# Hash-masked attention and two feed-forward blocks: the first head's operands loaded twice and written by the engines

## The chip, the cores and the metric

The kernel runs on one core of a Trainium2 chip. The core has TensorE (PE in the profile), VectorE (DVE), ScalarE (ACT), GpSimd (POOL) and SyncE (SP), each with its own instruction stream, and 16 DMA engines. Here SP and ACT issue the DMAs; the profile calls their queues q1 and q10. The metric is the device time of one execution in microseconds. The kernel before took 683.12 us (median of 3 runs, 682.26 to 685.02).

## The reference

All is computed in float32; some weights come as float64 and are converted in the kernel. Shapes: batch 2, 8 heads, 768 positions, 64 per head; model width 512.

```
q_bits = (q @ proj > 0);  k_bits = (k @ proj > 0)          # proj: 64 x 6, six sign bits
mask   = q_bucket[:, None] == k_bucket[None, :]            # the six bits as one number
scores = where(mask, q @ k.T / 8, -1e9)
attn   = exp(scores - max);  attn /= sum(attn) + 1e-9
x      = attn @ v                                          # 2 x 768 x 512, heads side by side
h = relu(x @ w_in);  u, v = halves of h;  v = layernorm(v)
y = (u * (w_spatial @ v + b_spatial)) @ w_out
out = y + relu(layernorm(y) * g_ln @ w_ch1) @ w_ch2
```

## The kernel before

TensorE multiplies float32 values in the format fp32r, and most operands are held as a pair, a high part (the value rounded to fp32r) and a low part (the rest), so that a product takes two or three passes.

Attention goes head by head. Two heads make a pair (`pair_load`, line 651): their keys and queries are loaded as 128 rows (two heads of 64) by 768 columns. `mismatch` (line 681) multiplies the raw pair by `sides`, a small matrix of `proj` with both signs (line 588), on PE into `pm`, and VectorE turns the signs into the mask rows `m`. `pair_split` (line 663) makes high and low parts. `passes_of` (line 703) assembles the operands of a single head: `ks`, 128 rows by two passes by 768 columns, and `qs`, the same by 384 columns (a group of three query tiles). Rows 0 to 63 and 64 to 127 hold different parts of the same head, and the second pass ends in 12 rows of mask. `passes_of` fills them by DMA from SBUF to SBUF; for the first head only, the mask rows are cast by VectorE (`first=True`). Then, for each tile of 128 queries: `scores` (four matmuls over 768 keys), `masked_max` on VectorE, `exps` on ScalarE, `transposes` on PE with copies `e` back to SBUF, and, per group, `weighted` (the product with the values `vv`).

Beside the attention, `conversions` loads float64 weights in pieces of 512 KB on ScalarE's queue (`stage_f64`: `f_out`, `f_v`, `f_u`) and converts them on ScalarE, VectorE and GpSimd. The first feed-forward block of batch 0 (`moe1`) lies in the attention's last part, and the rest of both blocks follows it.

The order is not written by hand. `Plan` records every operation as a job; `run` (line 281) simulates the engines with the costs in `cost` (line 220) and two DMA queues, twelve rounds, and `issue` emits the best order in time. A change of one job's cost or one job's place can thus reorder instructions far away. All recorded operations show line 478 of the profile's kernel (480 after the change).

Ahead of the first scores the kernel issues warming transposes of the identity matrix (`WARM` and `WARM2`, 24 and 12; their results are not used).

Of the kernel before, what the change touches and what calls it, by code (L numbers as in the profile page):

```python
# [9 lines left out]
F32 = mybir.dt.float32  # L10
F32R = mybir.dt.float32r
# [154 lines left out]
class Plan:  # L166
# [7 lines left out]
    LOOK = 60  # L174
    EARLY = 20.0
    ROUNDS = 12
    HOP = {"PE": 0.15, "ACT": 0.06, "DVE": 0.06, "POOL": 0.06, "SP": 0.05}
# [42 lines left out]
    def cost(self, engine, op, writes, reads, kw, job):  # L220
# [10 lines left out]
        if engine == "PE":  # L231
            if op == "transpose":
                return 0.109, 0.165
            if reads[0].dtype == F32:
                return n * (0.00083 if out.rows == 64 else 0.00042) + 0.006 + (0 if job.calls else 0.2), 0.2
            return n * 0.4375e-3 + 0.0065, 0.17
# [44 lines left out]
    def run(self, late=None):  # L281
# [20 lines left out]
        def opened(j):  # L302
            i = bisect_left(reached, j.at - self.LOOK)
            if i == len(reached):
                return None
            return max(when[i], late[j] - self.EARLY) if late else when[i]

# [176 lines left out]
def attn_moe_kernel(ctx: ExitStack, tc: tile.TileContext, qT, kT, v, proj, w_in, w_spT, b_sp, w_out, g_ln, w1, w2, out):  # L484
# [28 lines left out]
    WSE = (5, 3)  # L513
    WARM = 24
    WARM2 = 12
    XB = 3
# [65 lines left out]
    pj = const.tile([P, NB], F32, name="pj")  # L582
    nc.sync.dma_start(out=pj, in_=proj.rearrange("(o d) n -> o d n", o=1).to_broadcast([2, D, NB]))

# [5 lines left out]
    for a, own in enumerate((slice(0, D), slice(D, P))):  # L590
        for i, sign in enumerate((1.0, -1.0, 1.0)):
            at = a * HROW + i * NB
            nc.gpsimd.tensor_scalar(sides[own, at : at + NB], pj[own], sign, 0.0, op0=ALU.mult, op1=ALU.add)
    side = {"k": sides[:, NB : NB + QUAD], "q": sides[:, 0:QUAD]}
# [107 lines left out]

    def passes_of(nm, b, h, sl, first):

# [14 lines left out]
        for lo, hi in ((0, GW), (GW, S)):  # L719
            lo, hi = max(sl.start, lo), min(sl.stop, hi)  # L720
            if lo < hi:
                at = (2 * "kq".index(nm) + lo // GW) * QUAD + h % 2 * HROW
                rows = pr["m"][at : at + NM, lo % GW : lo % GW + hi - lo].bitcast(F32)
                to = t[D:MR, 1, lo - sl.start : hi - sl.start]
                if first:
                    nc.vector.tensor_copy(to, rows)
                else:
                    nc.sync.dma_start(out=to.bitcast(F32), in_=rows)
        return t

    def head_prep(b, h, first=False):
        heads[b, h] = {"ks": passes_of("k", b, h, slice(0, S), first)}

# [4 lines left out]

    def group_prep(b, h, g, first=False):
        groups[b, h, g] = {"qs": passes_of("q", b, h, slice(g * GW, (g + 1) * GW), first)}  # L740

# [335 lines left out]
    if WARM:  # L1077
        warm = ps_b.tile([P, P], F32, tag="b", name="warm")
        for _ in range(WARM):
            nc.tensor.transpose(warm, ident, ident)  # L1080
    pair_load(0, 0, first=True)
    mismatch(0, 0)
    pair_split(0, 0, first=True)
    head_prep(0, 0, first=True)
    group_prep(0, 0, 0, first=True)
    for _ in range(WARM2):
# [218 lines left out]
```

## Time and profile before

| | |
|---|---|
| time of the profiled execution | 684.13 us |
| its span, first to last instruction | 682.3 us |
| median of 3 runs (lowest, highest) | 683.12 us (682.26, 685.02) |
| busy: PE, DVE, ACT, POOL | 660.7, 433.0, 301.8, 197.2 us |
| mean granted clock of TensorE | 0.992 of 2.4 GHz |
| DMA | 84.36 MB, mean 124 GB/s |

A row of a timeline gives the start in us from the span's start, the length, the engine (a `q` behind the name: its DMA issues), and in brackets how long the engine had been idle and what ended that. Matmul lengths are latencies; several overlap. A row of stretches gives busy time per engine (PE, weight loads, DVE, ACT, POOL, each with a count), the granted clock, the busy share of the 16 DMA engines, and GB/s.

### The profile page before, as it was taken

The page shows a single profiled execution, that of the slowest core. Times are in us where ns is not written, and L with a number is a line of the kernel's source. Part 1 is how long each engine was busy: PE and PEld are TensorE (multiplying, and loading weights), DVE is VectorE, ACT ScalarE, POOL GpSimd, SP SyncE. Part 2 cuts the span into 40 slices and gives each one's busy share as a digit, 9 for nine tenths or more (in the row PEclk, how much of TensorE's full clock was granted, in tenths as well). Part 3 has the DMA queues.
Part 4 walks back from the last instruction along what each step waited for, and adds up shares of the span by engine and source line. Part 5 has one row for each costly group of instructions (what it writes and reads, how often), then busy time and mean ns, then how long its engine had stood idle before and what let it go on. Part 6 is the DMA issues. An engine that isn't in the chain of part 4 may idle for free. (4 is left out here: it accounts for less than half of the span.)

```text
span 682.3 us, 10207 instructions
## 1 busy us (share of the span) xinstructions
PE 660.7 (97%) x3772; PEld 537.6 (79%) x3772; DVE 433.0 (63%) x802; ACT 301.8 (44%) x591; POOL 197.2 (29%) x189
## 2 busy tenths in 40 slices
PE   6999999999999999999999999899999999999997
PEld 5887777878888788887688788688888878888886
DVE  2879787988657554534799686799888861112112
ACT  1887787767555545533464333433333221111110
POOL 2333433344432521100244241154554430000000
PEclk9899999999999999999999999899999999999999
DMA  7585765757546742624525440732332310002001
GB/s 195 133 212 139 186 176 147 191 122 193 175 92 218 217 117 73 226 121 162 186 80 216 137 133 33 263 113 89 106 92 93 93 61 1 0 1 92 1 1 61
DMA packets 47546, 84.36 MB, mean 124 GB/s; under 512 B 5678, under 2 KB 32010, under 8 KB 46474
## 3 DMA queue, kind: packets, MB, share of 16 engines
q1 hardware_dynamic: 34458, 54.36, 28.2%
q10 hardware_dynamic: 13040, 29.36, 13.2%
q8 instruction: 30, 0.49, 0.3%
q14 instruction: 18, 0.15, 0.1%
HBM read 51.12 MB, written 12.58 MB: 93 GB/s over the span
## 5 line engine op out<-in xcount | busy, mean ns | idle before, releaser
L478 PE MATMUL pc<-xh,w1t 128*128 128x512 f32 x576 | 143.9, 396 | 0.2 <-DVE xh L478 0.2
L478 PE MATMUL acc<-w2t,ch 128*128 128x512 f32 x576 | 141.9, 393 | 0.4 <-POOL w2t L478 0.4
L478 PEld LDWEIGHTS pc<-xh,w1t 128*128 128x128 f32 x576 | 108.4, 189 | 25.9 <-DVE xh L478 0.9
L478 PEld LDWEIGHTS acc<-w2t,ch 128*128 128x128 f32 x576 | 107.8, 188 | 25.0 <-POOL w2t L478 0.7
L478 ACT ACTIVATE x<-x,nb 128x768 f32<-128x768 f32 x96 | 89.6, 934 | 42.1 <-DVE x L478 38.2
L478 PE MATMUL sc<-ks,qs 128*128 128x512 f32 (+3 forms) x384 | 97.4, 372 | 7.7 <-DMA qs<-q 6.3
L478 DVE TENSOR_SCALAR_CACHE_REDUCE x<-sc 128x768 f32<-128x768 f32 x96 | 91.2, 953 | 19.5 <-PE sc L478 12.3
L478 DVE SCALAR_TENSOR_TENSOR ch<-pc,ch 128x512 fp32r<-128x512 f32 x48 | 33.0, 688 | 104.9 <-ACT ch L478 104.7
L478 PE MATMUL pt<-ident,x 128*128 128x128 f32 x576 | 82.7, 275 | 0.8 <-ACT e L478 0.5
L478 ACT ACTIVATE ch<-pc 128x512 fp32r<-128x512 f32 x48 | 28.7, 597 | 123.8 <-PE pc L478 123.4
L478 PEld LDWEIGHTS sc<-ks,qs 128*128 128x128 f32 (+1 forms) x384 | 65.2, 196 | 21.9 <-DMA qs<-q 7.2
L478 PEld LDWEIGHTS pt<-ident,x 128*128 128x128 f32 x576 | 66.9, 141 | 13.2 <-issue 3.1
L478 PE MATMUL po<-e,vv 128*64 128x192 f32 x768 | 69.5, 330 | 1.1 <-ACT e L478 1.1
L478 ACT ACTIVATE e<-pt 128x384 f32<-128x384 f32 x120 | 56.0, 484 | 31.4 <-PE pt L478 30.5
L478 POOL TENSOR_TENSOR f64c_w<-f_w,f64c_w 128x512 f32<-128x512 f32 x32 | 44.5, 1392 | 74.3 <-DVE f64c_w L478 70.9
L478 PEld LDWEIGHTS po<-e,vv 128*64 128x64 f32 x768 | 52.3, 137 | 12.4 <-issue 2.2
L478 DVE COPY e<-pt 128x384 f32<-128x384 f32 x72 | 39.7, 553 | 28.0 <-PE pt L478 27.7
L478 DVE TENSOR_SCALAR f64c_w<-f64c_w 128x512 f32<-128x512 f32 x64 | 40.7, 636 | 12.4 <-ACT f64c_w L478 11.4
L478 ACT ACTIVATE f64c_w<-f_w 128x512 f32<-128x512 f32 x32 | 21.5, 672 | 57.0 <-DMA f_w<-in_w 53.5
L478 PE MATMUL pg<-vn,w_sp 128*128 128x512 f32 x180 | 44.5, 399 | 0.0
L478 PEld LDWEIGHTS pg<-vn,w_sp 128*128 128x128 f32 x180 | 33.1, 188 | 8.0 <-issue 0.6
L478 DVE SCALAR_TENSOR_TENSOR f_w<-f_w,f64c_w 128x512 uint32<-128x512 uint32 x32 | 37.2, 1161 | 0.7
(125 smaller groups left out, 788.3 us busy)
## 6 DMA issues: line engine op xcount, KB each, us to landing
f_w<-in_w ACTq DMA_DIRECT2D x32, 512.0 KB
ks<-k SPq DMA_DIRECT2D x48, 192.0 KB
qs<-q SPq DMA_DIRECT2D x32, 192.0 KB
wst_sp<-in_w_spT SPq DMA_DIRECT2D x12, 384.0 KB
w_out<-ws_out SPq DMA_DIRECT2D x2, 2048.0 KB
qs<-q SPq DMA_DIRECT2D x32, 96.0 KB
vv<-in_v SPq DMA_DIRECT2D x16, 192.0 KB
ot<-y_dram SPq DMA_DIRECT2D x12, 256.0 KB
```

Source lines behind the costliest of these rows:

```text
L478: getattr(getattr(nc, engine[j.engine]), op)(*map(live, args), **{k: live(x) for k, x in kw.items()})
```

## The change

For the first head the parts are no longer copied from SBUF to SBUF. A new tile `dup` is loaded from DRAM: in its upper 64 partitions the first head's keys, and in both halves the first group's queries. ScalarE, VectorE and GpSimd write `ks` and `qs` in place from `k_raw` and `dup` (`first_parts`). The projection `pj` is issued by ScalarE instead of SyncE, and `sides` is written by VectorE instead of GpSimd. There are 24 warming transposes instead of 36, and the planner's cost of one is 0.213 instead of 0.109. A large DMA on ScalarE's queue may not be planned before 14.0 us (`BULK`).

```
@@ -173,6 +173,7 @@
     EARLY = 20.0
+    BULK = 14.0
     ROUNDS = 12
     HOP = {"PE": 0.15, "ACT": 0.06, "DVE": 0.06, "POOL": 0.06, "SP": 0.05}
     NEXT = 0.03
@@ -230,7 +231,7 @@
         psum = any(isinstance(x, View) and x.base.ring.pool.psum for x in (out, *reads))
         if engine == "PE":
             if op == "transpose":
-                return 0.109, 0.165
+                return (0.109 if isinstance(reads[0], View) else 0.213), 0.165
             if reads[0].dtype == F32:
                 return n * (0.00083 if out.rows == 64 else 0.00042) + 0.006 + (0 if job.calls else 0.2), 0.2
             return n * 0.4375e-3 + 0.0065, 0.17
@@ -303,7 +304,8 @@
             i = bisect_left(reached, j.at - self.LOOK)
             if i == len(reached):
                 return None
-            return max(when[i], late[j] - self.EARLY) if late else when[i]
+            bulk = self.BULK if j.engine == "ACT" and j.bytes > 200000 else 0.0
+            return max(when[i], bulk, late[j] - self.EARLY) if late else max(when[i], bulk)
 
         def done(j):
             stack = [j]
@@ -511,8 +513,8 @@
     VNP = [(0, t) for t in range(6)]
     UAT = {1: (0,), 2: (1,), 3: (2,), 5: (3, 4, 5)}
     WSE = (5, 3)
-    WARM = 24
-    WARM2 = 12
+    WARM = 16
+    WARM2 = 8
     XB = 3
     AT = (-10, -7, -6, -4, 0)
     PO = 2
@@ -580,7 +582,7 @@
     NM = 2 * NB
     MR = D + NM
     pj = const.tile([P, NB], F32, name="pj")
-    nc.sync.dma_start(out=pj, in_=proj.rearrange("(o d) n -> o d n", o=1).to_broadcast([2, D, NB]))
+    nc.scalar.dma_start(out=pj, in_=proj.rearrange("(o d) n -> o d n", o=1).to_broadcast([2, D, NB]))
 
 
     HROW = 3 * NB
@@ -590,7 +592,7 @@
     for a, own in enumerate((slice(0, D), slice(D, P))):
         for i, sign in enumerate((1.0, -1.0, 1.0)):
             at = a * HROW + i * NB
-            nc.gpsimd.tensor_scalar(sides[own, at : at + NB], pj[own], sign, 0.0, op0=ALU.mult, op1=ALU.add)
+            nc.vector.tensor_scalar(sides[own, at : at + NB], pj[own], sign, None, op0=ALU.mult)
     side = {"k": sides[:, NB : NB + QUAD], "q": sides[:, 0:QUAD]}
 
     above = const.tile([P, 1], F32, name="above")
@@ -700,7 +702,7 @@
     groups = {}
     tiles = {}
 
-    def passes_of(nm, b, h, sl, first):
+    def passes_of(nm, b, h, sl):
 
 
 
@@ -722,22 +724,48 @@
                 at = (2 * "kq".index(nm) + lo // GW) * QUAD + h % 2 * HROW
                 rows = pr["m"][at : at + NM, lo % GW : lo % GW + hi - lo].bitcast(F32)
                 to = t[D:MR, 1, lo - sl.start : hi - sl.start]
-                if first:
-                    nc.vector.tensor_copy(to, rows)
-                else:
-                    nc.sync.dma_start(out=to.bitcast(F32), in_=rows)
+                nc.sync.dma_start(out=to.bitcast(F32), in_=rows)
         return t
 
-    def head_prep(b, h, first=False):
-        heads[b, h] = {"ks": passes_of("k", b, h, slice(0, S), first)}
+    def first_load():
+        dup = ap.tile([P, NKT, GW], F32, tag="e", name="dup", bufs=EB)
+        nc.sync.dma_start(out=dup[D:P, 0:2], in_=kT[0, 0].rearrange("d (a s) -> d a s", a=2))
+        nc.sync.dma_start(
+            out=dup[:, 2], in_=qT[0, 0, :, 0:GW].rearrange("(o d) s -> o d s", o=1).to_broadcast([2, D, GW])
+        )
+        return dup
+
+    def first_parts(dup):
+        pr = pairs[0, 0]
+        k_raw = pr["k", "raw"]
+        ks = ap.tile([P, 2, S], F32R, tag="ks", name="ks_0_0_0", bufs=2)
+        qs = ap.tile([P, 2, GW], F32R, tag="qs", name="qs_0_0_0", bufs=QB)
+        nc.scalar.activation(ks[0:D, 1], k_raw[0:D], AF.Copy)
+        nc.vector.tensor_tensor(ks[0:D, 0], k_raw[0:D], ks[0:D, 1].bitcast(F32), op=ALU.subtract)
+        split_hi(ks[D:P, 0].rearrange("d (a s) -> d a s", a=2), dup[D:P, 0:2])
+        nc.scalar.activation(qs[:, 0], dup[:, 2], AF.Copy, scale=-SCALE)
+        nc.vector.scalar_tensor_tensor(
+            qs[D:P, 0], dup[D:P, 2], -SCALE, qs[D:P, 0].bitcast(F32), op0=ALU.mult, op1=ALU.subtract
+        )
+        nc.vector.tensor_copy(qs[0:D, 1], qs[0:D, 0])
+        heads[0, 0], groups[0, 0, 0] = {"ks": ks}, {"qs": qs}
+        for n, to in enumerate((ks[D:MR, 1, 0:GW], ks[D:MR, 1, GW:S], qs[D:MR, 1])):
+            rows = pr["m"][n * QUAD : n * QUAD + NM].bitcast(F32)
+            if n == 1:
+                nc.scalar.activation(to, rows, AF.Copy)
+            else:
+                nc.vector.tensor_copy(to, rows)
+
+    def head_prep(b, h):
+        heads[b, h] = {"ks": passes_of("k", b, h, slice(0, S))}
 
     def head_prep3(b, h):
         vv = ap.tile([P, NKT, D], F32, tag="vv", name=f"vv_{b}_{h}", bufs=2)
         nc.sync.dma_start(out=vv, in_=v[b, :, h])
         heads[b, h]["vv"] = vv
 
-    def group_prep(b, h, g, first=False):
-        groups[b, h, g] = {"qs": passes_of("q", b, h, slice(g * GW, (g + 1) * GW), first)}
+    def group_prep(b, h, g):
+        groups[b, h, g] = {"qs": passes_of("q", b, h, slice(g * GW, (g + 1) * GW))}
 
     def scores(b, h, g, j):
         jm = f"{b}_{h}_{g}_{j}"
@@ -1079,10 +1107,10 @@
         for _ in range(WARM):
             nc.tensor.transpose(warm, ident, ident)
     pair_load(0, 0, first=True)
+    dup = first_load()
     mismatch(0, 0)
+    first_parts(dup)
     pair_split(0, 0, first=True)
-    head_prep(0, 0, first=True)
-    group_prep(0, 0, 0, first=True)
     for _ in range(WARM2):
         nc.tensor.transpose(warm, ident, ident)
     head_prep3(0, 0)
```

The planner then orders VectorE's first instructions differently. Before, in the stretch up to the first masked maximum (`x`); `k_0_0` and `q_0_0` are the pair's split parts, `ks`, `qs` the first head's operands:

```order
L478 SCALAR_TENSOR_TENSOR k_0_0_144<-k_raw,k_0_0_144 128x768
L478 SCALAR_TENSOR_TENSOR q_0_0_158<-q_raw,q_0_0_158 128x768
L478 TENSOR_SCALAR m_0_179<-pm_0_172,above,worth 128x384
L478 CAST ks_0_0_154<-m_0_179 12x384 x2
L478 CAST qs_0_0_166<-m_0_179 12x384
L478 TENSOR_SCALAR x_0_0_0_199,nb_0_0_0_198<-sc_0_0_0_189 128x768
```

After:

```order
L480 TENSOR_SCALAR sides<-pj 64x6 x6
L480 SCALAR_TENSOR_TENSOR q_0_0_141<-q_raw,q_0_0_141 128x768
L480 TENSOR_TENSOR ks_0_0_157<-k_raw,ks_0_0_157 64x768
L480 TENSOR_SCALAR m_0_172<-pm_0_159,above,worth 128x384
L480 SCALAR_TENSOR_TENSOR qs_0_0_151<-dup,qs_0_0_151 64x384
L480 COPY qs_0_0_151<-qs_0_0_151 64x384
L480 CAST ks_0_0_157<-m_0_172 12x384
L480 CAST qs_0_0_151<-m_0_172 12x384
L480 SCALAR_TENSOR_TENSOR k_0_0_165<-k_raw,k_0_0_165 128x768
L480 TENSOR_SCALAR x_0_0_0_193,nb_0_0_0_192<-sc_0_0_0_183 128x768
```

`sides` and three instructions that write the first head's parts have come in; the split of the queries now stands ahead of that of the keys, which has gone behind the casts.

SyncE's queue from its first issue. Before (`qs_0_384` is the second query group of the first head, `ks_1_0` the second head's keys):

```order
L478 DMA k_raw<-in_kT 128x768
L478 DMA q_raw<-in_qT 128x768
L478 DMA pj<-in_proj 128x1x6
L478 DMA ks_0_0_154<-k_0_0_144 64x768 x3
L478 DMA qs_0_0_166<-q_0_0_158 64x2x384
L478 DMA qs_0_384_169<-q_0_0_158 64x2x384
L478 DMA qs_0_0_166<-q_0_0_158 64x384
L478 DMA qs_0_384_169<-q_0_0_158 64x384
L478 DMA ks_1_0_181<-k_0_0_144 64x768
L478 DMA qs_0_384_169<-m_0_179 12x384
L478 DMA ks_1_0_181<-k_0_0_144 64x768 x2
L478 DMA ks_1_0_181<-m_0_179 12x384 x2
```

After:

```order
L480 DMA q_raw<-in_qT 128x768
L480 DMA k_raw<-in_kT 128x768
L480 DMA dup<-in_qT 128x1x384
L480 DMA dup<-in_kT 64x768
L480 DMA vv_0_127<-in_v 128x384
L480 DMA qs_0_384_152<-q_0_0_141 64x2x384
L480 DMA qs_0_384_152<-q_0_0_141 64x384
L480 DMA ks_1_0_170<-k_0_0_165 64x768 x2
L480 DMA qs_0_384_152<-m_0_172 12x384
L480 DMA ks_1_0_170<-m_0_172 12x384 x2
L480 DMA ks_1_0_170<-k_0_0_165 64x768
L480 DMA q_0_1_198<-in_qT 128x768
```

The copies into `ks_0_0` and `qs_0_0` are gone, the two loads into `dup` and the value load stand ahead of all copies, and `pj` has left the queue.

ScalarE's queue up to the second `e` copy. Before:

```order
L478 ACT_TABLE_LOAD
L478 ACTIVATE k_0_0_144<-k_raw 128x768
L478 ACTIVATE q_0_0_158<-q_raw 128x768
L478 DMA f_out_210<-in_w_out 128x1024
L478 ACTIVATE x_0_0_0_199,z_sum_214<-x_0_0_0_199,nb_0_0_0_198 128x768
L478 ACTIVATE x_0_0_1_205,z_sum_214<-x_0_0_1_205,nb_0_0_1_204 128x768
L478 ACTIVATE x_0_0_2_222,z_sum_214<-x_0_0_2_222,nb_0_0_2_221 128x768
L478 ACTIVATE e_0_0_254<-pt_0_0_0_0_230 128x3x128
```

After:

```order
L480 DMA pj<-in_proj 128x1x6
L480 ACT_TABLE_LOAD
L480 ACTIVATE q_0_0_141<-q_raw 128x768
L480 ACTIVATE ks_0_0_157<-k_raw 64x768
L480 ACTIVATE k_0_0_165<-k_raw 128x768
L480 ACTIVATE qs_0_0_151<-dup 128x384
L480 ACTIVATE ks_0_0_157<-m_0_172 12x384
L480 ACTIVATE x_0_0_0_193,z_sum_206<-x_0_0_0_193,nb_0_0_0_192 128x768
L480 ACTIVATE x_0_0_1_201,z_sum_206<-x_0_0_1_201,nb_0_0_1_200 128x768
L480 ACTIVATE e_0_0_228<-pt_0_0_0_0_219 128x3x128
L480 DMA f_out_238<-in_w_out 128x1024
L480 ACTIVATE x_0_0_2_216,z_sum_206<-x_0_0_2_216,nb_0_0_2_215 128x768
```

The `pj` load comes first, three copies for the first head have come in, and the first weight load (`f_out`) has moved behind two exponentials and an `e` copy.

## Rows read from the trace of the kernel before

**Rows 1.** The page: TensorE's busy time; its granted clock in 40 slices:

```profile
PE 660.7 (97%) x3772; PEld 537.6 (79%) x3772; DVE 433.0 (63%) x802; ACT 301.8 (44%) x591; POOL 197.2 (29%) x189
...
PEclk9899999999999999999999999899999999999999
```

**Rows 2.** TensorE's waits, whole run: total, times, longest (us):

```profile
PE sc L478 <- DMA qs<-q: 6.3, 2, 5.3
PE px_c L478 <- ACT xc L478: 2.8, 1, 2.8
```

**Rows 3.** TensorE's timeline: start, length, instruction, count, idle before:

```profile
1.45 6.78 PE L478 MATMUL warm<-ident 128*128 128x128 f32 x36 [1.45 <-POOL above L478]
8.16 0.52 PE L478 MATMUL pm<-k_raw,sides 128*32 128x384 f32 x2
...
14.31 5.64 PE L478 MATMUL sc<-ks,qs 128*128 128x512 f32 x16 [5.30 <-DMA qs<-q]
19.75 1.21 PE L478 MATMUL pt<-ident,x 128*128 128x128 f32 x6
```

**Rows 4.** Stretches: length, busy per engine, granted clock, DMA share, GB/s:

```profile
9.10:13.60 4.50, 0.00 (x0) 0.00 (x0) 1.73 (x4) 0.00 (x0) 0.00 (x0) 1.00 1.10 213
13.75:20.50 6.75, 6.19 (x20) 5.36 (x21) 2.90 (x6) 2.79 (x5) 0.00 (x0) 0.50 0.54 121
20.60:38.40 17.80, 17.77 (x146) 14.46 (x144) 14.94 (x30) 14.57 (x36) 7.39 (x6) 1.00 0.68 179
437.00:440.30 3.30, 3.19 (x12) 2.90 (x13) 2.80 (x6) 3.30 (x7) 0.00 (x0) 0.50 0.51 195
```

**Rows 5.** TensorE by lines, 1.4 to 6.8 us: count, busy, mean ns:

```profile
L478 PE MATMUL warm<-ident 128*128 128x128 f32 x25 | 5.6, 423 | 1.4 <-POOL above L478 1.4
```

**Rows 6.** ScalarE's timeline at the start and near 436 us:

```profile
3.67 0.84 ACT L478 ACTIVATE k<-k_raw 128x768 fp32r<-128x768 f32 x1 [1.66 <-DMA k_raw<-in_kT]
4.62 0.84 ACT L478 ACTIVATE q<-q_raw 128x768 fp32r<-128x768 f32 x1
4.63 0.41 ACTq L478 DMA_DIRECT2D f_out<-in_w_out  x1
...
25.05 0.68 ACT L478 ACTIVATE f64c_out<-f_out 128x512 f32<-128x512 f32 x1
...
435.78 0.66 ACT L478 ACTIVATE f64c_w<-f_w 128x512 f32<-128x512 f32 x1 [3.66 <-DMA f_w<-in_w]
```

**Rows 7.** GpSimd's timeline at the start:

```profile
4.89 2.58 POOL L478 TENSOR_SCALAR sides<-pj 64x6 f32<-64x6 f32 x6 [1.45 <-DMA pj<-in_proj]
```

**Rows 8.** VectorE's timeline at the start:

```profile
4.54 0.96 DVE L478 SCALAR_TENSOR_TENSOR k<-k_raw,k 128x768 fp32r<-128x768 f32 x1 [4.54 <-ACT k L478]
...
9.17 0.68 DVE L478 TENSOR_SCALAR m<-pm,above,worth 128x384 fp32r<-128x384 f32 x1 [2.71 <-PE pm L478]
9.88 0.72 DVE L478 CAST ks<-m 12x384 fp32r<-12x384 f32 x2
...
16.00 0.96 DVE L478 TENSOR_SCALAR_CACHE_REDUCE x<-sc 128x768 f32<-128x768 f32 x1 [5.04 <-PE sc L478]
```

**Rows 9.** DMA issues on SyncE's queue at the start:

```profile
4.54 1.81 SPq L478 DMA_DIRECT2D ks<-k  x3
```

**Rows 10.** Stretches at the start, for DMA share and GB/s:

```profile
2.40:3.80 1.40, 1.40 (x8) 1.40 (x7) 0.00 (x0) 0.13 (x1) 0.66 (x8) 1.00 1.01 404
4.00:4.20 0.20, 0.20 (x3) 0.20 (x2) 0.00 (x0) 0.20 (x1) 0.00 (x0) 1.00 0.38 98
4.20:4.33 0.13, 0.13 (x3) 0.13 (x2) 0.00 (x0) 0.13 (x1) 0.00 (x0) 1.00 0.20 8
4.34:4.49 0.15, 0.15 (x3) 0.15 (x2) 0.00 (x0) 0.15 (x1) 0.00 (x0) 1.00 0.10 4
9.40:13.40 4.00, 0.00 (x0) 0.00 (x0) 1.50 (x4) 0.00 (x0) 0.00 (x0) 1.00 1.10 208
```

**Rows 11.** GpSimd by lines: the split of one pair's keys:

```profile
L478 POOL TENSOR_SCALAR k<-k 128x768 fp32r<-128x768 f32 x7 | 6.1, 869 | 25.7 <-DMA k<-in_kT 18.4 <-DMA qs<-q 6.2 <-DMA qs<-m 1.2
```

## The prediction

> **What bounds the kernel now.** I read the page's first two parts, then the waits of TensorE (PE), then its timeline up to 21 us. PE is busy for 660.7 of 682.3 us [rows 1], so it idles 21.6 us in all, and a change helps if it removes idle time of PE or time that PE spends at its lower clock. The longest single wait is at the start: the score matmuls wait 5.3 us for the DMA copies of the first queries [rows 2]. The timeline shows the place: 36 warming transposes from 1.45 us, the four bit matmuls `pm` from 8.16 us, nothing after about 9.0, and the first scores at 14.31 [rows 3]. Once it is over its start-up, PE is busy for 17.77 of the next 17.80 us [rows 4], so what starts earlier can end earlier.
>
> The same gap costs a second time. The granted clock is 1.00 until 13.6 and 0.50 from 13.75 to 20.5 us [rows 4], that is 1.2 GHz of 2.4: it fell after PE had stood idle since 9.0, and the first sixteen score matmuls and six transposes ran at that level. It fell once more at 437 us, after PE's 2.8 us wait for `xc` [rows 2, 4]. Before 6.9 us the clock column has no record of the lower level, but the transposes have: 25 of the 36 start between 1.45 and 6.8, one per 0.214 us, and the other 11 in the next 1.3 [rows 3, 5].
>
> **The change, part by part.** The sum goes from the last warming transpose to the first scores.
>
> Warming. 24 transposes instead of 36; all 24 are at the slow pace, 24 x 0.214 = 5.1 us, so `pm` can start at 1.45 + 5.1 = 6.6 instead of 8.16. It needs `sides` and both raw tiles by then. The raw tiles were in ACT's hands at 3.67 and by 4.6 [rows 6]; queries now come first, which swaps the two. `sides` now needs no POOL: the six tiny instructions that took POOL from 4.89 to 7.47 [rows 7] run on DVE, with `pj` issued by ACT at the start and not third on SP. Even at the pace on POOL (2.58 us in all), and `pj` landing no earlier than before, they would be done at 7.5, 0.9 later than 6.6; with `pj` no longer behind two issues on SP (an issue takes 0.41 [rows 6]), by 6.6. I take 6.6 and keep 0.9 as the bad end. Then `pm` (8.16 to 9.0) ends at 7.5, and `m`, which followed 1.0 after `pm`'s start and takes 0.68 [rows 8], is written from 7.6 to 8.3. That is 1.6 us ahead of before.
>
> The first head's parts. Before, three copies of keys and two of the queries went from SBUF to SBUF on SP's queue from 4.54 on [rows 9], among the next heads' copies, and the last of them ended PE's wait. They go. In their place engines write the parts out of `k_raw` and the new tile `dup`. The critical one is the query half of `dup`: 128 rows of 384 floats, 197 KB, read with a leading broadcast of two. `pj` was read in the same way, and while only `pj` was moving (4.20 to 4.33 us) the DMA share was 0.20, so at most 3.2 of 16 engines worked on it [rows 10]. I take two engines, one per copy. A full load moved 404 GB/s at a share of 1.01, 25 GB/s per engine [rows 10]; 197 KB / 2 / 25 = 3.9 us. On 16 engines it would be 0.5 us; at the pace of the SBUF copies (208 GB/s at 1.10, 11.8 GB/s per engine) 8.3 us. Its source is DRAM, as that of the full load, so 3.9 is the nearest. It queues behind the raw loads, whose bytes end at about 4.1 (98 GB/s are left from 4.0 to 4.2 [rows 10]), so it ends at 8.0 and reaches its waiter some 0.4 later, as `pj` did (last bytes about 4.5 [rows 10], POOL at 4.89 [rows 7]): 8.4.
>
> The Trainium skill says the same and more sharply: "DMA: Bandwidth & Descriptors", section "Rules for kernel authors", has it that an outermost dimension of c copies confines a transfer to at most c engines, and the trace of `pj` agrees as far as its share can tell. By that rule the engines are two and the load 3.9 us; without it 0.5.
>
> From 8.4: ACT's copy of 128x384 (half of the 0.84 of 128x768 [rows 6]) 0.45, to 8.85; DVE's subtraction of 64x384 (half of 0.96 [rows 8]) 0.5, to 9.35; DVE's copy of 64x384, 0.35 to 0.5, to 9.75; two 12-row casts at 0.35 [rows 8], to 10.45. The third cast is on ACT beside them. The upper keys come from the second half of `dup`, queued behind the first on the slow engines: 0.5 later, 8.9, plus POOL's 0.87 for 768 columns [rows 11], 9.8, inside the same span. So the first score matmul starts at 9.8 and the second, which needs the casts, at 10.55, against 14.31: **3.75 us earlier**.
>
> After that DVE has the keys' subtraction (0.96) still before the first masked maximum: 10.45 to 11.4. The scores need about 1.3 us more (at the lower clock the first tile took 14.31 to 16.00), so that subtraction is hidden; the maximum starts at about 11.85 instead of 16.00 [rows 8], **4.15 us earlier**. If its cover went, it would cost what it sticks out, at most 1 us.
>
> The clock. PE's idle time before the scores shrinks from 5.3 us to about 2.3 plus 0.5 between its first two score matmuls. If the clock stays at 2.4 GHz, the sixteen score matmuls and six transposes, 6.4 us at half speed, need 3.2; but DVE's maxima (0.96 each, two score buffers) and ACT's exponentials then set the pace, and following the chain maximum, exponential, transposes by these durations I get the state of 20.7 us at about 15.1: 5.6 earlier. If the clock falls as before, the shift is the 4.15. An idle time of 2.8 us was enough once [rows 2, 4], so I take it to fall more often than not, and put **4.4** between them.
>
> Weights. The first `f_out` load (512 KB) leaves ACT's queue at 4.63 [rows 6] and now comes after the first exponentials and the first `e` copy, at about 15. It no longer competes with the first copies. Its first use, `f64c_out` at 25.05 [rows 6], moves to about 20; the load needs its 1.3 us at full rate, 2.6 if shared, so it lands near 18 to 19. That is covered; if not, ACT's queue holds exponentials behind the waiting instruction, up to 1 us. The value load goes to SP's fifth place and costs nothing: it stood behind the first scores.
>
> Queue behind. SP's later copies for the second query group and second head wait behind the slow `dup` load on two engines, to about 12 or 13. They are wanted at 13.5 and 18. Covered by 0.5 or more.
>
> The rest. From 20.6 on PE has 14.85 us of idle time left (21.6 less 1.45 and 5.3), in many small waits and one of 2.8 at 434 [rows 1, 2]. There ACT has the weight word `f64c_w`, which waits for its load until 435.78, ahead of the scaling of `xc` [rows 6]; the changed order still has it ahead. The planner reshuffles the remainder; I give that 0, plus or minus 1.
>
> **Sum.** 4.4 us off the profiled execution, whose time is 684.13 (span 682.3): 679.7. That execution lies 1.0 above the median, 683.12, so I expect 683.12 - 4.4 = 678.7 as the median, rounded to **678.8**.
>
> **Rivals.**
> *The scores start as forecast and the clock does not fall, or `dup` spreads wider.* For it: only some 2.5 us of idle time are left. Against it: the fall at 437. The gain is 5.6 to 7, about 676.9.
>
> *The gain is used up downstream.* Scores start near 10.5, but `f64c_out` waits for its later load with the exponentials behind it, or SP's copies for the next tiles come late from the two crowded engines. For it: the load loses 10 us of lead, and a single late copy cost PE 5.3. Against it: fewer copies share the engines than before. 1 to 2.5 us go back: about 681.3, within 0.5%.
>
> *Slower: the `dup` load is the new wait.* If its two engines move it at the pace of the copies, 8.3 us instead of 3.9, it reaches ACT at 12.8 and the scores start at 14.95; everything queued behind on SP is 4.4 later too. It decides from 7.7 us of load on, where the start of the scores is again 14.31. 0.65 at the start and 1 to 2 for the late copies give about 685.5. Against it: the rate of the loads from DRAM.
>
> *The change doesn't do what it says.* DVE's order might put the first casts behind something late; the order shows them directly behind the copy, so it has no chance of its own.
>
> **How the numbers follow.** Forecast 0.58, with a range of its own of 677.3 to 680.4 (the 4.15 and 5.6, and the reshuffling). Better 0.20, used up 0.18, slower 0.04. About 0.5% (3.4 us) is what a measurement here can tell from no change: faster means below 679.7. Of the forecast's share I put 0.46 below it and 0.12 above; with 0.20 of the better case faster has 0.66. Same has 0.12 + 0.17 + 0.01 = 0.30, slower 0.04. To hold eight in ten the range reaches into both neighbours: 676.2 to 681.6.
>
> **What would show it.** In the profile after: `pm` at about 6.6 and `m` ending near 8.3; the first score matmul near 9.8, waiting for DVE or POOL and no longer for `qs<-q`; a DMA share of about 0.1 to 0.2 from 5 to 8 us; the first maximum at 11 to 12; whether the clock is 0.50 between 10 and 20. Wrong would be: scores before 8.5 (then `dup` was spread), scores after 13 (then it was slower than a load), a new wait of ACT for `f_out`, or a start as forecast with an end less than 3 us earlier.

## The result, and the profile after

The changed kernel takes **693.07 us** (median of 4 runs, 690.85 to 695.53), the kernel before 683.73 beside it: ratio 1.0144, 95% interval 1.0122 to 1.0166. It is 1.4% slower. I had said 678.8, range 676.2 to 681.6, with 0.04 for slower. One execution of E9 below (931.63 us) and one of the kernel before beside E13 to E16 (1314.53 us) lie far off all others and are left out of every comparison.

The profiled execution took 695.53 us (span 693.3). First PE's timeline at the start (start, duration, instruction, in brackets the idle time ahead and what ended it); it answers to [rows 3]:

```profile
6.55 0.52 PE L480 MATMUL pm<-k_raw,sides 128*32 128x384 f32 x2 [0.38 <-DVE sides L480]
...
12.18 0.79 PE L480 MATMUL sc<-ks,qs 128*128 128x512 f32 x1 [4.78 <-POOL ks L480]
13.21 4.75 PE L480 MATMUL sc<-ks,qs 76*128 76x512 f32 x13 [0.24 <-DVE qs L480]
```

The bit matmuls start at 6.55, as forecast; the first scores at 12.18 and 13.21 where I had 9.8 and 10.55. ACT's timeline, beside [rows 6], and DVE's, beside [rows 8], say what they waited for:

```profile
10.32 0.52 ACT L480 ACTIVATE qs<-dup 128x384 fp32r<-128x384 f32 x1 [3.20 <-DMA dup<-in_qT]
...
18.65 0.36 ACTq L480 DMA_DIRECT2D f_out<-in_w_out  x1
...
23.29 0.67 ACT L480 ACTIVATE f64c_out<-f_out 128x512 f32<-128x512 f32 x1
```

```profile
5.85 0.64 DVE L480 TENSOR_SCALAR sides<-pj 64x6 f32<-64x6 f32 x6 [5.85 <-DMA pj<-in_proj]
...
8.27 0.66 DVE L480 TENSOR_SCALAR m<-pm,above,worth 128x384 fp32r<-128x384 f32 x1
...
11.46 0.88 DVE L480 CAST qs<-qs 64x384 fp32r<-64x384 f32 x1
12.35 0.35 DVE L480 CAST ks<-m 12x384 fp32r<-12x384 f32 x1
12.71 0.35 DVE L480 CAST qs<-m 12x384 fp32r<-12x384 f32 x1
...
14.44 0.96 DVE L480 TENSOR_SCALAR_CACHE_REDUCE x<-sc 128x768 f32<-128x768 f32 x1 [0.39 <-PE sc L480]
```

ACT idles 3.20 us for the doubled query load, until 10.32 (forecast 8.4); DVE's copy of 64x384 takes 0.88 while POOL works on the upper keys (forecast 0.35 to 0.5). The first maximum starts at 14.44, 1.56 before that of [rows 8], not 4.15. The later weight load costs nothing: ACT runs `f64c_out` at 23.29 without a wait.

So the start is earlier than before, by less than I said, and still the kernel is slower. Stretches of the kernel after (length, busy time of PE, PEld, DVE, ACT and POOL with instructions, granted clock, DMA share, GB/s):

```profile
7.50:8.50 1.00, 0.00 (x0) 0.00 (x0) 1.00 (x2) 0.00 (x0) 0.00 (x0) 1.00 0.13 46
12.17:19.00 6.83, 6.58 (x21) 5.25 (x21) 4.72 (x10) 2.42 (x5) 0.78 (x1) 0.50 0.40 107
83.85:87.26 3.41, 3.41 (x23) 2.38 (x19) 0.73 (x3) 1.22 (x4) 0.70 (x1) 0.50 1.02 244
445.66:452.49 6.83, 4.89 (x16) 3.70 (x16) 4.22 (x10) 4.75 (x8) 0.00 (x0) 0.50 0.57 219
```

From 7.5 to 8.5 us, with only the doubled load moving as I read it, the share is 0.13: two of sixteen engines. The clock is at its lower level for 6.83 us at the start, as long as in [rows 4], only 1.6 us earlier. Where before had 3.3 us of it at 437 us, here 6.83 stand at 446, and one at 84 us is new. PE's longest waits (total, times, longest), beside [rows 2]:

```profile
PE sc L480 <- POOL ks L480: 4.8, 1, 4.8
PE sc L480 <- DMA qs<-q: 2.1, 2, 1.9
PE px_c L480 <- ACT xc L480: 1.9, 1, 1.9
PE pt L480 <- ACT x L480: 1.9, 3, 1.1
PE sc L480 <- DMA ks<-k: 1.7, 1, 1.7
PE sc L480 <- DVE f64c_u L480: 1.6, 1, 1.6
```

The 5.3 us for `qs<-q` at the start has become 4.8 for `ks`, and below stand waits of 1 to 2 us in the middle of the program that, but for the one for `xc`, before did not have. Three stretches of before, after, and experiment E1 (below), in this order, show where PE lost time:

```profile
34.00:90.00 56.00, 54.03 (x449) 44.00 (x445) 45.66 (x99) 44.20 (x100) 22.72 (x22) 1.00 0.67 176
90.00:200.00 110.00, 107.72 (x822) 87.86 (x821) 88.53 (x190) 77.40 (x168) 41.64 (x41) 1.00 0.60 156
430.00:460.00 30.00, 27.00 (x121) 21.61 (x120) 25.17 (x42) 13.54 (x23) 10.30 (x8) 0.94 0.50 171
```

```profile
34.00:90.00 56.00, 51.72 (x418) 42.34 (x420) 42.55 (x92) 42.94 (x96) 19.46 (x19) 0.97 0.71 176
90.00:200.00 110.00, 103.46 (x796) 82.94 (x790) 87.34 (x182) 74.79 (x161) 41.42 (x40) 1.00 0.58 154
430.00:460.00 30.00, 26.51 (x121) 21.19 (x120) 21.04 (x44) 12.43 (x21) 6.69 (x5) 0.89 0.56 193
```

```profile
34.00:90.00 56.00, 55.24 (x465) 45.44 (x464) 48.91 (x103) 45.27 (x101) 22.79 (x21) 1.00 0.69 179
90.00:200.00 110.00, 108.57 (x827) 88.59 (x825) 86.46 (x186) 76.66 (x167) 43.58 (x42) 1.00 0.60 160
430.00:460.00 30.00, 29.71 (x134) 23.92 (x133) 28.55 (x41) 12.62 (x23) 14.39 (x11) 1.00 0.41 138
```

PE idled 2.0 of 56 us and 2.3 of 110 us before, 4.3 and 6.5 after. The loss builds up step by step: at the same PE instructions the kernel after is 2.1 us ahead of before at the first scores, 0.7 behind at 42 us, 3.0 at 91, 8.3 at 184 and 11.2 at 438. Nothing that the diff names happens there. What differs is the order: the planner gave the 2516 jobs recorded behind the start (the same jobs in both kernels) another order on every engine.

### The profile page after: what moved, and what is told of

Read it like the earlier page. It is cut to its first block, busy times and chain, and to the rows that moved or that the text cites. A ratio compares the mean times of both kernels' runs of the same rounds, so it can differ in the third digit from the quotient of the medians.

```text
span 693.3 us, 10186 instructions
## 1 busy us (share of the span) xinstructions
PE 663.1 (96%) x3760; PEld 536.4 (77%) x3760; DVE 432.7 (62%) x810; ACT 304.9 (44%) x594; POOL 196.7 (28%) x184
## 5 line engine op out<-in xcount | busy, mean ns | idle before, releaser
L480 POOL TENSOR_TENSOR f64c_w<-f_w,f64c_w 128x512 f32<-128x512 f32 x32 | 46.0, 1439 | 79.9 <-DVE f64c_w L480 72.8
L480 DVE TENSOR_SCALAR f64c_w<-f64c_w 128x512 f32<-128x512 f32 x64 | 35.8, 559 | 18.0 <-ACT f64c_w L480 17.5
L480 ACT ACTIVATE f64c_w<-f_w 128x512 f32<-128x512 f32 x32 | 21.5, 670 | 54.0 <-DMA f_w<-in_w 51.1
L480 PE MATMUL pv<-w_v,act_x 128*128 128x512 f32 x144 | 36.9, 399 | 1.8 <-ACT vr L480 0.7
```

The source lines that it names most:

```text
L480: getattr(getattr(nc, engine[j.engine]), op)(*map(live, args), **{k: live(x) for k, x in kw.items()})
```

## The experiments

**Theory 1**: the loss lies in that order alone. **Theory 2**: the new start makes it (the two-engine load, the backlog on the queues, the later weight load). To part them I give those jobs the order of the other kernel: a table holds each job's planned start, and the program is emitted by it, as far as dependencies allow.

```
-        order = sorted((j for j in self.jobs if j.engine), key=lambda j: (j.part, j.start, j.at))
+        real = [j for j in self.jobs if j.engine]
+        for j, at in zip(real[-len(PIN):], PIN):
+            j.start = at / 100
...
+            _, _, j = heappop(heap)
+            if j.engine:
+                order.append(j)
```

**E1**, changed start, old order.

> The changed start (two extra loads, parts written in place, projection on ACT, 16 and 8 warming transposes) with every one of the 2516 jobs behind the start issued in the order of the kernel before. Theory 1 (the loss lies in the planner's new order of those jobs): 680 to 684 us, no slower than before: the first scores stay near 12.2 us instead of 14.3, some of that lead is kept, and PE's idle time between 34 and 195 us goes back from 10.7 to about 4 us. Theory 2 (the new start itself, by its loads and the backlog it leaves, costs the time): 689 to 694 us, with the same waits between 34 and 195 us as in the changed kernel.

**E2**, old start, new order.

> The mirror image: the start of the kernel before with the 2516 later jobs in the order of the changed kernel. Theory 1: 690 to 695 us, with waits of PE near 82, 135, 158 and 163 us as in the changed kernel, and the low clock near 84 us. Theory 2: 682 to 685 us, as before.

(The ratio is that to the kernel before measured beside the run, with its 95% interval.) E1: **676.44 us**, ratio 0.9921 [0.9892, 0.9951]. E2: 693.47, 1.0163 [1.0119, 1.0207]. The new order costs what the changed kernel costs whichever start stands ahead of it; with the old order the changed start is faster than before, and by more than I had expected of E1 (680 to 684). So the two-engine load and the backlog are out as causes. The weight load is one of the 2516 jobs and moves with their order, so these two runs don't part it from the order; E6 and E7 below do: the first `f_out` load leaves at 10.06 us in E6, near E1's 9.87, and at 20.24 in E7, and both are slower than before.

**E4**, the kernel before with the planner nudged: is any other order worse?

```
-    LAND = 1.13
+    LAND = 1.14
```

> The kernel before with one number of the planner changed by 1% (LAND 1.13 to 1.14 us, the time it books for a transfer's landing); no instruction is added, taken away or resized. Theory 1 says that the order alone moves the time by per cents: a time that differs from before by more than 2 us, either way, likely slower (686 to 695 us). Theory 2 has nothing in it that moves: 682 to 685 us.

683.75, 1.0012 [0.9993, 1.003]: no change, though its trace shows another order on every engine. My "likely slower" was wrong. **E8** is the same edit on the changed kernel.

> The changed kernel with the planner's LAND at 1.14 instead of 1.13 us; the work is the same, the order of the rest is planned anew, as different from both kernels' orders as these are from each other, and planned to end at 664.45 us (the changed kernel's 664.66). If an order's time hangs on chance (theory 1, in the form that the plan can't tell good orders from bad ones): a time that is away from 693.07 by more than 3 us, anywhere between 676 and 700 us; I take 685. If the changed start makes every order that is planned for it bad: 690 to 696 us.

686.94, 1.0065 [1.004, 1.009]: 6 us under the changed kernel with the same work in it. So orders are not all alike, that of the changed kernel is a bad one, and a new order need not be worse than the old one.

**E3**, E1 with the query load spread, and **E5**, the same edit with the new order:

```
-            out=dup[:, 2], in_=qT[0, 0, :, 0:GW].rearrange("(o d) s -> o d s", o=1).to_broadcast([2, D, GW])
...
+        nc.sync.dma_start(out=dup[0:D, 2], in_=qT[0, 0, :, 0:GW])
+        nc.sync.dma_start(out=dup[D:P, 2], in_=qT[0, 0, :, 0:GW])
```

> As the kernel with the new start and the old order, but the doubled query load is made by two loads of 64 rows each instead of one load with a leading broadcast. If the two DMA engines that carried it are what held the start (ACT waited 3.20 us for it, to 10.32), it reaches ACT by about 8.7 us, and the first scores start at 10.3 to 11 instead of 12.18. The whole: 2 us less than the kernel without this edit if that lead is kept (678 to 682 us); the same within 1 us if it is lost at the second pair's keys near 39 us. If the load's spread is not what holds the start, the first scores stay near 12.2.

> The changed kernel with its own order of the 2516 later jobs, and only the doubled query load made by two loads of 64 rows. With the old order this edit brought the first score from 11.86 to 9.35 us. The changed kernel's order was planned for a first score at 9.93 us, which came at 12.18. Theory 1a (the order is bad by itself, whenever the start ends): 689 to 692 us, at most the 2.8 us of the earlier start better than the changed kernel's 693.07. Theory 1b (the order is good, but only for a start that keeps to the plan): 677 to 683 us, with the waits of PE at 82, 135, 158 and 163 us gone.

E3: 676.21, 0.9931 [0.9903, 0.996]. PE's timeline there:

```profile
9.35 0.77 PE L637 MATMUL sc<-ks,qs 128*128 128x512 f32 x1 [2.12 <-DVE qs L637]
10.46 5.18 PE L637 MATMUL sc<-ks,qs 76*128 76x512 f32 x15 [0.35 <-DVE qs L637]
```

First scores 2.5 us earlier than in E1: the two-engine load did hold the start. The whole is no faster than E1's 676.44. What held E3's start in its place, on ACT and DVE:

```profile
6.83 0.51 ACT L637 ACTIVATE qs<-dup 128x384 fp32r<-128x384 f32 x1
```

```profile
8.65 0.56 DVE L637 SCALAR_TENSOR_TENSOR qs<-dup,qs 64x384 fp32r<-64x384 f32 x1
```

The load is there when ACT comes to it at 6.83, and DVE, busy without a break since 5.54 with `sides`, two splits and `m`, comes to it at 8.65. E5: 689.4, 1.0094 [1.0058, 1.0129]. A start that comes before the planned 9.93 does not make the new order good.

**E6** and **E7** cut the table at 60 us of planned time; **E16** gives the new order to the two last stages only (from about 300 us).

> The changed start; jobs planned before 60 us in the order of the kernel before, all others in the changed kernel's order. Against the kernel with the old order throughout (676.44), the changed kernel was behind by 3 us at 41 us of the trace, by 7 at 90, by 9 at 140, by 14 at 190 and by 20 at the end of its profile. Theory 1a as losses place by place: only the first 3 us come back, so 687 to 691 us. Rival (the whole loss starts at the second pair's keys near 39 us and the rest follows from it): 677 to 681 us.

> The mirror image: jobs planned before 60 us in the changed kernel's order, all others in the order of the kernel before. Losses place by place: 678 to 681 us, 3 us over the kernel with the old order throughout. Rival (the loss starts near 39 us and the rest follows): 688 to 693 us.

> The changed start, all jobs of the attention stage (to about 300 us) in the order of the kernel before, those of the two last stages in the changed kernel's. The kernel with the old order throughout took 676.44, the one with the new order from 60 us on 687.54. If the last two stages' order costs its share of the profiles' difference (PE busy 125.4 of 130 us and 26.5 of 30 there, against 126.2 and 29.7): 680 to 682 us. If their order is indifferent and only the lateness of the stage before is carried into them: 676 to 678 us.

E6: 687.54, 1.0069 [1.0037, 1.0102]. E7: 686.12, 1.0045 [1.0023, 1.0067]. E16: 683.54, 1.0016 [0.9994, 1.0037]. Over E1 these are 11.1, 9.7 and 7.1 us by the medians, where the whole new order is 16.6 over it (15 by the ratios): both parts of E6 and E7 cost, and they do not add up. E7 fell between its two expectations, E16 above both of its own. E16 keeps a riddle: in its profile PE was already 5.8 us behind E1's at 140 us, long before the first place where their orders differ (about 330 us); another 3.9 came behind that place. A part of the 5.8 is clock:

```profile
9.26:19.50 10.24, 6.78 (x21) 5.56 (x22) 6.02 (x12) 4.08 (x9) 0.84 (x1) 0.50 0.53 137
132.14:135.55 3.41, 3.41 (x16) 2.65 (x16) 3.17 (x8) 2.81 (x7) 1.30 (x1) 0.50 0.65 167
```

That is 13.65 us at the lower level, where E1 has 6.83 (from 10.18 to 17.01), and is worth 3.4 us at most. What makes the rest stays open, so the 7.1 can't be put down to the last stages' order alone.

**E9**, **E10**, **E13**: single places of the new order mended. E9 moves one POOL join behind the two key pieces, E10 three query loads ahead of the next pair's raw loads, E13 does both; the edits of E9 and E10 change 1 and 3 numbers of the table (dependencies let E10's loads pass the query load only, not the key load ahead of it):

```
-26.55 (k piece), 25.25 (join f64c_out)
+26.55 (k piece), 26.56 (join f64c_out)
...
-64.48, 65.09, 65.70 (qs loads), 63.58, 64.03 (raw loads)
+63.55, 63.56, 63.57 (qs loads), 63.58, 64.03 (raw loads)
```

> The changed kernel with one instruction moved: POOL's first join of f64c_out, which its order puts between the two pieces of the second pair's split keys (29.62 and 32.56 us), stands behind both, as in the kernel before. The second piece should run 2 us earlier, SP's ks load behind it be issued at about 32.4 instead of 34.37, and PE's wait of 1.74 us at 39.10 for that load go. If what is lost here is lost for good: 690.5 to 692 us (1.7 less than the changed kernel's 693.07). If the next wait swallows it: 692.5 to 693.5, with the later waits longer.

> The changed kernel with three SP loads moved: the qs loads of the third pair's second head stand ahead of the fourth pair's raw key and query loads (786 KB), not behind them. In the changed kernel these two were issued at 75.36 and 75.72 us, after SP had waited 2.6 us for their buffer, the qs loads at 76.69, and PE waited 1.95 us at 82.26 for them; its clock was then 0.50 from 83.85 to 87.26. Expected: that wait gone, the low clock with it, and 2 to 3.6 us less: 689.5 to 691 us. If it is given back by the fourth pair's keys coming later: 692 to 694.

> The changed kernel with both moves at once: POOL's join behind both pieces of the second pair's keys, and the three qs loads ahead of the fourth pair's raw loads. If the waits of 1.74 us at 39.10 and 1.95 us at 82.26 and the low clock behind the second are lost for good where they stand: both gone from the trace, and 688 to 690 us. If what is saved at one is spent at the next: 691 to 693 us, with PE's busy time between 34 and 90 us up from 51.7 to 54 and that between 90 and 200 us no higher than 103.5.

E9: 691.49, 1.0142 [1.0106, 1.0177], without a profile that can be compared. E10: 692.45, 1.0151 [1.0114, 1.0188]. E13: 693.85, 1.0163 [1.0133, 1.0192]. None differs from the changed kernel. PE's waits at the two places, in E13 (the changed kernel waited for the load at 39.10) and in E10 (the changed kernel waited at 82.26):

```profile
40.70 1.35 PE L637 MATMUL sc<-ks,qs 128*128 128x512 f32 x4 [2.44 <-DVE f64c_out L637]
```

```profile
81.04 0.97 PE L637 MATMUL sc<-ks,qs 128*128 128x512 f32 x4 [1.05 <-DVE x L637]
```

The loads no longer end them; DVE does, after 2.44 us where it was 1.74 and after 1.05 where it was 1.95. Mending the wait that a profile names is not mending the order.

**E11**, **E14**: does PE's idle time ahead of the scores bring the low clock, and what does that cost? Both start from E3 and put warming transposes behind the bit matmuls, E11 through `WARM = 23`, `WARM2 = 9` and a planned start for the second lot, E14 by hand:

```
+        j = [j for j in real[: -len(PIN)] if j.engine == "PE" and j.kind[0] == "transpose"][-1]
+        j.start, j.calls = 8.0, j.calls[:1] * 18
```

> The kernel with the new start, the spread query load and the old order (676.21), and of its warming transposes 23 ahead of the four pm matmuls and 9 behind them, instead of 24 ahead and none behind, so that PE is busy from 7.2 to about 9.3 us, where it waited 2.12 us for the first scores. In the kernel without this edit the granted clock fell to 0.50 at about 9.7 us and stayed there to 16.9. If that idle time is why it fell: the clock stays at 1.00 through the first score matmuls, the 16 of them take about 3 us instead of 5.2, and the whole is 1.5 to 3.4 us shorter, 673 to 675 us. If it falls all the same: 676 to 677.

> The kernel with the new start, the spread query load and the old order (676.21), every engine's order as there, but 22 warming transposes ahead of the pm matmuls and 18 behind them. Nine of them took 1.20 us behind pm, so 18 should keep PE busy from 7.2 to about 9.5 us. If the clock falls after the wait of 2.12 us for the first scores because PE stood idle: the granted clock stays at 1.00 through the first scores, and the first 16 score matmuls take 3 to 3.5 us instead of 5.2; 673 to 675 us. If the clock falls all the same, now or a little later: 675 to 677 us.

E11: 680.03, 0.9966 [0.994, 0.9993]; its planner put a third split ahead of the mask on DVE, the scores came at 10.89 after 2.6 us of idle time, and the clock fell, so it does not answer the question. E14: 678.29, 0.9936 [0.9914, 0.9958]. E14's PE timeline, and the stretch after it:

```profile
7.08 2.18 PE L639 MATMUL warm<-ident 128*128 128x128 f32 x18
9.41 0.47 PE L639 MATMUL sc<-ks,qs 128*128 128x512 f32 x1
10.53 1.42 PE L639 MATMUL sc<-ks,qs 76*128 76x512 f32 x7 [0.64 <-DVE qs L639]
12.30 1.85 PE L639 MATMUL sc<-ks,qs 128*128 128x512 f32 x8 [0.35 <-DVE x L639]
```

```profile
9.40:16.00 6.60, 5.59 (x33) 4.54 (x33) 5.70 (x13) 3.44 (x8) 0.00 (x0) 1.00 0.73 177
```

With PE busy from 7.08 to 9.2 us the clock stays at 1.00 (2.4 GHz), where E3 had 0.50 from 9.34 to 16.16. But the whole is not faster than E3, and above what I expected in either case (673 to 677). Now the scores wait for DVE (the maxima, before 12.30), and PE's third group of `po` starts at 36.4 us, in E3 at 36.3. At the start the lower clock is covered. (Behind that E14's profile loses 4.9 us on E3's, 3 of them near 430 us, where PE waits 2.8 us for `xc` and the clock falls once more. Why is open; it says nothing on the start.)

**E12**, only the small edits, old order; **E15**, the spread load with the planner's own order for it.

> The kernel before in its own order, with only the small edits of the start: 24 warming transposes instead of 36, the projection loaded by ACT first, its sides written by DVE. Neither the doubled loads nor the parts written in place. The pm matmuls start at about 6.6 us instead of 8.16; the query parts still go through their SP loads, and the first scores start between 12.8 and 14.3. If the doubled loads and the parts in place are what makes the start short in the old order: 681 to 683 us. If the small edits alone do it: 676 to 679.

> The changed kernel with the query load spread over two loads and nothing else, and the order that the planner makes for it. The start is the good one (first score near 9.4 us). If a plan made for a good start is good: 676 to 680. If the planner's orders scatter by chance, with the four seen so far (old 676.4 on the new start, nudged old 683.75 on the old start, new 689.4 on the spread start, nudged new 686.9) as the sample: 677 to 690, I take 683.

E12: 680.99, 0.9985 [0.9959, 1.001], not to be told from before: the doubled loads and the parts written in place carry most of the gain, if not all. E15: 686.49, 1.0074 [1.0045, 1.0102]. A plan made for the good start came out 10 us over the old plan on the same start (E3).

**E17** and **E18** are E1 and E3 once more, side by side.

> The kernel with the changed start and the old order once more, in another set of runs and beside the one with the spread load. If the order carries the loss: 675 to 680 us again, 0.5% or more under the kernel before. If those four runs were lucky and the kernel with the new order only behind 300 us (683.54) shows the true level of this start: 681 to 684 us.

> The kernel with the spread query load and the old order, side by side with the one without the spread. Its first score starts 2.5 us earlier in the profile. If that lead reaches the end: 2 to 2.5 us faster than its neighbour. If it is swallowed, as the 3 us that PE saved by the full clock at the start were by 36 us: the same within 1 us; 675 to 679 us.

677.17, 0.992 [0.9892, 0.9948], and 675.86, **0.9908 [0.9875, 0.9941]**. The gain of the old order holds: both versions beat both kernels. Of the spread's 2.5 us at the start 1.3 are left between these two medians (0.2 between E1's and E3's), within the scatter of the runs.

**What in the order does it (read, not tried).** The weights' conversions run among the attention work: an ACT load of 512 KB, ACT's first step, DVE's steps, POOL's join. One piece in the changed kernel, on ACT, DVE and PE:

```profile
126.56 0.34 ACTq L480 DMA_DIRECT2D f_u<-in_w_in  x1
...
133.31 0.66 ACT L480 ACTIVATE f64c_u<-f_u 128x512 f32<-128x512 f32 x1 [2.39 <-DMA f_u<-in_w_in]
133.88 0.92 ACT L480 ACTIVATE x<-x,nb 128x768 f32<-128x768 f32 x1
```

```profile
134.00 0.89 DVE L480 TENSOR_SCALAR f64c_u<-f64c_u 128x512 f32<-128x512 f32 x2 [2.59 <-ACT f64c_u L480]
```

```profile
132.18 1.64 PE L480 MATMUL sc<-ks,qs 128*128 128x512 f32 x6
134.95 0.55 PE L480 MATMUL pt<-ident,x 128*128 128x128 f32 x3 [1.13 <-ACT x L480]
```

The load is issued at 126.56. The planner books 0.4 for the issue, 1.13 for the landing and 524,288 / 250e3 = 2.1 for the bytes, 3.6 us in all, and puts ACT's step where the load is then due. On the chip it is there at 133.31, after 6.75 us. ACT idles 2.39 with the next exponential (`x`, 133.88) queued behind that step; DVE idles 2.59; PE idles 1.13 for that `x`. This load is the slowest of its kind: of the twelve in this profile all but the first reach ACT's step after 3.8 to 6.8 us, in E1's after 3.9 to 5.6, so with the good order too they come later than booked. The waits of conversion steps from 34 to 200 us, of the kernel after and of E1:

```profile
DVE f64c_u L480 <- ACT f64c_u L480: 6.7, 3, 3.6
ACT f64c_u L480 <- DMA f_u<-in_w_in: 6.6, 3, 3.3
...
DVE f64c_out L480 <- ACT f64c_out L480: 2.2, 2, 1.6
...
DVE f64c_v L480 <- ACT f64c_v L480: 1.7, 2, 1.4
...
ACT f64c_v L480 <- DMA f_v<-in_w_in: 1.3, 2, 0.9
```

```profile
DVE f64c_u L637 <- ACT f64c_u L637: 2.8, 2, 1.6
...
ACT f64c_v L637 <- DMA f_v<-in_w_in: 2.5, 3, 1.2
...
ACT f64c_u L637 <- DMA f_u<-in_w_in: 1.3, 1, 1.3
```

In sums from 34 to 460 us of each profile, with all of PE's waits there and the profiled time:

| kernel | DVE's conversion steps waited for ACT | PE waited | us |
|---|---|---|---|
| E3 | 5.6 | 5.7 | 673.47 |
| E1 | 5.3 | 5.9 | 675.38 |
| E12 | 8.6 | 7.9 | 679.96 |
| before | 11.5 | 10.0 | 684.13 |
| E8 | 13.2 | 11.2 | 686.70 |
| E7 | 12.0 | 11.0 | 687.41 |
| E6 | 16.0 | 14.1 | 687.43 |
| E15 | 12.9 | 13.9 | 688.18 |
| E5 | 21.7 | 18.2 | 688.50 |
| E2 | 19.3 | 18.5 | 696.31 |
| after | 21.5 | 18.6 | 695.53 |

Over all 19 comparable profiles the first column and the time have a rank correlation of 0.92. That is a correlation over orders that were not made to test it: a conversion step may be late because everything is, and PE's waits, the loss itself, go with the time at 0.97. One link of the chain fails the same test: ACT's conversion steps waited for their loads 17.6 us in the kernel after, 19.4 in E1 and 26.6 in the kernel before, and over the 19 profiles that sum goes against the time (-0.59). (The loads of the attention's weights alone, from 34 to 200 us, go with it at 0.56.) So late loads alone do not tell a bad order from a good one, whatever they did at 126 us. No run changed the booked rate or moved these steps alone: what in the order does it stays open.

## Why the prediction was wrong

**The step that failed is "The rest":** "The planner reshuffles the remainder; I give that 0, plus or minus 1". It was worth +16.6 us (changed kernel 693.07 against E1's 676.44; 15 by the ratios to the kernel before). E1 and E2 show that it is the order; what in it costs the time is open. I had the evidence in the two orders, which differ on every engine far behind the start, and priced it as noise without a row for it. It also moved the sign: the cases on the slower side had 0.04 between them.

**Warming, bit matmuls, `m`**: the bit matmuls started at 6.55 against 6.6, in part by luck: `pj` came to DVE only at 5.85, later than to POOL before (4.89), but DVE wrote `sides` in 0.64 us and not in 2.58. `m` ran from 8.27 to 8.93 against an end of 8.3, since DVE ran two splits ahead of it.

**The doubled query load**: the mechanism was right, two engines, as I had taken from the broadcast of `pj`: the share is 0.13 from 7.5 to 8.5 us. The Trainium skill, "DMA: Bandwidth & Descriptors", section "Rules for kernel authors", has it that a leading broadcast of c copies confines a transfer to at most c engines; this trace agrees with its 0.13. The size was off: it reached ACT at 10.32, not 8.4. Alone on its engines it kept nearly to my 25 GB/s per engine (46 / (0.13 x 16) = 22 from 7.5 to 8.5 us), so the 1.9 us were lost ahead of that, where I take it that other loads shared its two engines. E3, with it spread, starts its scores at 9.35 and 10.46, close to my 9.8 and 10.55, but not for my reason: its load is there by 6.83, and DVE's work ahead, which my sum let end with `m` at 8.3, holds the start until 8.65. From there on my terms hold.

**DVE and POOL**: the copy of 64x384 took 0.88 while POOL worked (0.35 in E3, where POOL had ended), the upper keys 11.08 to 12.13 instead of 8.9 to 9.8. With the load, the lead was 1.1 us at the second score matmul, not 3.75, and 1.56 at the first maximum, not 4.15: these terms were mis-sized, but E1 and E17, which have the same start, are faster than before all the same.

**The clock**: it fell, as I held likelier, but the value I gave a clock that stays up was wrong in kind. E14 kept it up: against E3, 0.7 us was left of that at 25 us and nothing by 36. The range I gave the forecast by itself, 677.3 to 680.4, does not follow from its terms either: 4.15 to 5.6 off the median is 677.5 to 679.0, with 1 us for the reshuffling 676.5 to 680.0.

**Weights, queue behind**: covered at the first use, as said; the changed kernel's later copies stand in the new order, so that term can't be read by itself.

**The rivals**: the slower one had the right sign through the wrong place. The load was late by part of what it asked, and that costs 2.5 us at the start; at the end nothing that the runs can tell (E17 and E18). With the old order the forecast's sign and nearly its size come out (676.4 and 677.2 against 678.8), but the size in part by luck: the start gave less than I said, and the gain grew along the way. E1's profile is 2.7 us ahead of that of before at 30 us, 5.4 at 310, and 9.2 at the end, where the wait for `xc` and the low clock behind it are gone, a wait that I had left as it was.

## What to carry to other kernels

Where a planner or scheduler sets the order, an edit anywhere is also a draw of a new order for everything behind it: price that draw from orders that have been timed (here 676 to 693 us for the same jobs), or pin the order (issue the jobs by a fixed table) and time the edit alone. If the pinned edit is good and the planned one bad, keep the old order as a table. Don't mend a bad order at the waits that the profile names one by one; the next operand ends the same wait.

## What was not expected of the hardware

- The load with the leading broadcast was late by amounts that differ: the first score matmul that waits for its data started between 11.86 and 12.48 us in the four profiles whose start has the old order and between 12.18 and 13.77 in five others, but between 9.33 and 9.56 in five with the load spread and the same order of the start.
- In those nine profiles DVE's copy of 64x384 ran while POOL wrote the upper keys and took 0.87 to 1.01 us; with the load spread POOL had ended before, and the copy took 0.35.
- One kernel's executions differ by several us. In E2 this goes with the low-clock stretches that they meet: 690.8 us twice at a mean granted clock of 0.995, 696.1 to 696.3 at 0.984 to 0.987. In E18 it doesn't: six executions between 674.52 and 679.53, all at 0.995. A single profile can be 3 us from the median; the profiled execution after, at 0.988, is one of the long ones.
